# Taps of the shift read in place as fp32, and all steps of a hand-scheduled kernel in another order

## Chip, cores and metric

One core of one Trainium2 chip. The time is device microseconds of one execution, and the median over runs is compared.

## The reference

Two blocks follow each other on one sequence of S = 2048 positions and D = 512 channels (F = 1792 in the MLP). Cut to what is computed:

```python
def _A_ref(q, k, v, shift_k, ssm_k, ssm_D):          # q is already normalised
    for t in range(4):                               # a shift of k by 0..3 positions, 4 taps per channel
        k_shift += k_pad[:, t:t + S, :] * shift_k[:, 3 - t]
    kv = k_shift * v
    y = irfft(rfft(pad(kv)) * rfft(pad(ssm_k)))[:S]  # a causal convolution as long as the sequence
    return q * (y + kv * ssm_D)

def _B_ref(x, w1, w2, w3, w4):
    h = gelu(layernorm(x) @ w1)
    hs = concat(four channel groups of h, moved by -1, +1, -2, +2 positions) @ w2
    x1 = x + hs
    return x1 + gelu(layernorm(x1) @ w3) @ w4

def reference(...):
    h = x + _A_ref(layernorm(x), A_k, A_v, A_shift_k, A_ssm_k, A_ssm_D)
    return h + _B_ref(layernorm(h), B_w1, B_w2, B_w3, B_w4)
```

Inputs and output are bf16. The four taps per channel, `shift_k`, are what the first part of the change is about.

## The kernel before

The kernel is a list of 812 steps. Each is added with a name, the engines that may run it with a planner's cost, the steps it depends on, and the buffers that it takes and gives back (`Plan.add`). A string `ORDER` lists them: a word such as `093P2` is step number 93, on engine P, in buffer 2. `emit` runs through it and issues each step's instructions. So `ORDER` alone sets, for each engine's queue, the order of its instructions, which of several possible engines a step is on, and which buffers it uses. Engines run their queues strictly in order; a step waits in its queue for what it depends on, and all behind it wait too. P is TensorE (PE), V is VectorE (DVE), A is ScalarE (ACT), G is GpSimd (POOL), and S is SyncE (SP), which issues every DMA. The SP queue goes round eight semaphores, so that a transfer is issued only when the one eight places before it has landed.

Positions are split in two halves s = 0, 1 of 8 blocks b of 128 partitions; channels in four chunks c of 128. PSUM has eight banks, handed out by number. The steps in the order of the computation, with their lines in the profile:

- Loads (L268): `Lf` the filter, `Lk` the shifted input k with the taps behind its columns, `Lv`, `Lq`, `Lw1` to `Lw4` the weights. `Lsd` (L273) and `dr` (L296) put `ssm_D` into the filter.
- `skf(c)` (L259, `copy`): casts the four bf16 taps of chunk c, from the last columns of the `Lk` tile in `r_k`, into an fp32 tile `sskf`. `dg(c)` (L309 on DVE, L307 on ACT): four multiplies of the identity by one tap each, which makes four diagonal matrices in `r_dg`.
- `K(g,c)` (L444): seven matmuls with the diagonal matrices, the shift. `KV(g,c)` (L452, DVE): times v.
- `bits` (L324 to L328, DVE), `cons` (L331 to L335, POOL), `ftv`, `fta`, `ft`, `ttv`, `tta`, `tts`, `f2v`, `f2a`, `f2s`: tables of sines, made from indices on POOL, DVE and, last, ACT (L346, L360, L368). `tt` and `f2` finish them on POOL.
- The convolution is a transform in two stages with matrices. `S1` (L391) and its copies out of PSUM `E1` (L259, ACT or DVE), a regrouping of partitions by DMA `X` (L407), `S2` (L415) and its copies `E2` (L259; L427 for the signal F1). The signals are F0, F1 (filter) and A0, A1 (kv). `P` (L476, DVE): products of two spectra in SBUF. `I2` (L486), copies `EV` (L259), DMA `XI` (L497) and `I1` (L504): the way back.
- `Q` (L508) statistics of q for the first layernorm; `QV` (L516 and after), `QP` (L531) and `QN` (L537): mean and inverse deviation on DVE or POOL. `Y` (L614, L616): q normalised, into one of two buffers `z_t`. `H` (L619, DVE): the gated sum h, read from the PSUM of `I1`.
- Per pair p of blocks: `HS` squares (L603 on ACT, L605 on DVE), `uw`, `rr`, `hn` (from L587 to L649) the two layernorm factors, `hb` (L656, L658) the normalised block, `LT` and `TE` its transpose (L673 on PE and a copy L259, or, for some pairs, out and back by DMA, L666 and L668), `W` (L702) times w1, `U` (L706) gelu.
- `X2` (L725) times w2 with the moved groups, `S` (L728), squares `SS` (L603, L605), `ux`, `r1`, `xn` (L587 to L595 and L748 to L759) the third layernorm, `lb` (L656, L658), `LX` and `EX` its transpose in the same two ways, `R` (L732) the residual.
- `M` (L780) times w3 and `G` (L784) gelu, seven of each per pair; `O` (L793) times w4, 14 matmuls per block; `Z` (L795) the last addition and `OUT` (L797) the store.

The taps and their use before:

```python
add(("skf", c), {V: 0.17, GP: 0.22, A: 0.22},
    lambda e, sl, c=c: copy(e, sskf[:, 4 * c:4 * c + 4], kw[:, 0, c, NB * 129:KW]), [("Lk", 0, c)])
...
sc = sskf[:, 4 * c + j:4 * c + j + 1]
...
add(("dg", c), {V: 0.8, A: 1.19, GP: 1.45}, dg(c), [("skf", c)], port="VG")
```

Of the kernel before, what the change touches and what calls it, by code (L numbers as in the profile page):

```python
# [9 lines left out]
P = 128  # L10
# [3 lines left out]
DC = D // P  # L14
FC = F // P
NB = 8
XW = 258
KW = NB * 129 + 4

BF16 = mybir.dt.bfloat16  # L20
F32 = mybir.dt.float32
# [7 lines left out]
SC = 2.0 * math.pi / 4096.0 * (1.0 - 2e-8)  # L29

ORDER = """
002S 004S 003S 005S 031V 041V 042G 043G 000S 029P0 030P 059P23 001S 007S 061P45 006S 062V 067P67 010S 033V 037V 032V 069P01 008S 070V 009S 060A 068A
034V 063P23 064A 065P45 066A 023S 049G 022S 038A 035V 091P60 039V 055P23 099P71 100V 036A 044V 056A 057P45 058A 040V 101P0 102V 103P1 104V 050V 045A
355V 051A 046G 047V 105P7 106V 048A 093P2 095P3 076S 119P45 120A 094V 115P01 354V 077S 054G 024S 075S 015S 096V 097P7 078S 116A 074S 073S 092V 098V
020S 071S 358V 121P23 122A 117P45 107P01 357V 053G 108A 118V 072S 111P67 113P23 021S 114V 016S 127S 109P01 112A 110A 123S 088P4567 089V 128S 090A
085P0123 087A 082P4567 083A 356V 086V 231P21 084A 079P4501 232V 124S 080V 081A 129S 125S 131P6723 130S 134P0145 132V 133A 136A 126S 144V0 143V1 352V
147V2 146V3 135A 014S 137P2367 019S 233P4 011S 139A 018S 145P01670 154V0 153V1 138A 148P 157V2 149A 156V3 223P50 224V 150A 155P01231 158P 159M 160A
187P67 353V 344S 229P5 234V 163V0 164V1 017S 151S 152S 230V 012S 351V 188A 140P0123 141A 235P4 142A 166V2 167V3 161S 162S 165P67010 168P 173V0 013S
359G 169A 174V1 227P5 170A 171S 172S 176V2 175P23671 177V3 178P 180A 199P01 228V 237P5 179V 236V 200A 181S 182S 238V 225P6 226V 343S 360G 361G 052A
362V0 191P23 193P01 192A 189P45 190A 194V 204S 203S 195P67 196A 201P23 202V 197P01 198A 183P45 239P67 365G1 366V 371G1 367A 207S 241P23 208S 184P01  # L40
363V 368G0 364A 242V 243P45 245P23 240A 369V 386G 372V 244A 246A 210S 373A 374V0 209S 206S 205S 257S 387G 185P67 247P01 377V1 375V 380G0 248A 378V
214P2345 215V 370A 249P67 250A 379A 388G 399V 186P01 381V 027S 255S 389G0 392G1 251P23 252A 253P67 254A 376A 383G1 390P00 393P2 259S 216V 211P4567
394V 391A 395P3 258S 384V 212V 382A 220P0145 400G 401G 402A2 405A3 403P21 404A 346S 213V 412G 413G 221V 406P6 397P7 347V 396A 263P0123 385A 398A 407V
265A 260S 222V 408P6 276V0 414G 415G0 416P72 264A 418G1 410P4 425V 426G 417A 411A 419P5 420V 217P0123 409A 275V1 423P7 424A 421P5 219V 277P67230 218V
279V2 427G 428G2 431G3 429P40 422A 534P5 430A 432P0 433A 278V3 535V 536A 282V0 530P1 531V 532A 256S 281V1 436P4 280P 284V2 434P5 435A 437A 285V3 283P
286P 287A 288A 586V 587G 292V0 588G 291V1 522P0 523V 524V 266P4567 526P1 527V 529V 268A 589G0 592G1 262S 590P01 538P2 593P3 594V 528A 537V 591A 542P6
543V 267A 595P70 596A 293P01451 607P3 345S 608A 599P6 603P7 295V2 601P3 539V 294V3 600A 025S 439V 296P 297V0 298V1 300V2 301V3 026S 299P 540A 307V0
544A 643G 442V 605P2 604A 302P 602A 644G 645G 649A2 646V3 597P6 606A 541V 308V1 303A 533V 615G 616G 598A 647P72 304A 443V 261S 269P0123 271V 270A
612P6 613V 272P4501 274V 289S 290S 311V2 310V3 650P2 651V 609P3 610V 648A 309P67010 652P20 312P 617V 653A 656P3 619A0 314V0 028S 445V 273A 657A 618V1
305S 306S 664P2 665A 313V1 316V2 317V3 315P 324V0 318P 319A 620S 654P4 323V1 621S 326V2 662P5 325P23671 327V3 330V0 329V1 622S0 328P 320A 321S 322S  # L50
658P0 663A 333V2 659A 660P1 614S 332V3 331P 661A 655A 438V 440V 444V 334P 335A 669P5 666P0 441V 446V 336A 337S 338S 339P14 623P20 447G 340P36 545V
629P7 448V 452V0 449G1 450V 451A 453V 624A 455G1 456V 341P14 458G0 459V 633P2 454A 473G 474G 631P3 625P6 460V 464A1 461A0 465V 457A 462V 463A 632A
475G 486V 476V3 479V2 635P4 630A 634A 477P11 627P3 466V 498V 348G 636A 478V 626A 470V1 480P7 481A 342P24 628A 487G 488G 482P6 489A1 471V 472A 467G0
468V 469A 490G0 499G 484P7 485A 510V 492S 483A 349V 640P1 491S 550P3 500G 502V3 504S 501A2 503S 493S2 511G 512V 514G0 551V 513A1 515S 546P4 637P2
494P7 496P6 552A 547V 548A 672G 549V 495A 516S 505S0 508P3 506P4 497A 509A 350G 507A 517S1 518P7 519A 520P6 673G 674G 675V3 677S 638V 521A 562P2 676V2
563V 566P3 564A 558P4 567V 554P7 568A 700V 574P6 701G 702G 703A1 704G0 678S 679S2 680P20 611S 705S 570P3 559V 560A 686P4 687A 555V 670V 688P7 692P5
681A 682P4 556V 690P2 575V 576V 553V 683A 684P6 685A 693A 756G 706S 757G 671S 758V 759V3 760G2 707S0 578P4 571V 572V 582P3 728G 729G 583V 730G 731G1
762S 584A 641V 761S 763S1 708P60 710P5 732V0 711A 691A 734S 579V 577V 569V 580V 784V 733S 735S2 785G 525V 557V 639S 720P3 561V 573V 714P1 718P4 719A
709A 764P50 765A 716P2 717A 772P4 766P6 712P5 713A 767A 786G 788G2 790S 787V3 789S 791S0 736P20 737A 768P5 689A 746P6 747A 738P2 739A 642S 774P7 773A
769A 776P6 744P2 667V 668S 777A 740P0 745A 792P40 748P5 796P6 793A 770P2 804P4 797A 800P6 749A 802P5 771A 741A 798P2 715A 801A 805A 803A 742P0 743A  # L60
794P1 694P6 753P4 799A 750P5 775A 778P0 781P2 782V 751V 783S 779V 780S 581V 795A 721A 754V 755S 565V 585V 697P7 698V 695V 699S 809P1 810V 811S 696S
722P3 723V 724S 806P2 807V 808S 725P5 726V 752S 727S
"""


class Plan:
# [28 lines left out]
def body(ctx, tc, fx, kt, q, v, sd, w1, w2, w3, w4, out):  # L95
# [34 lines left out]
    kw = r_k[:].rearrange("p (s c x) -> p s c x", s=2, c=DC)  # L130
# [123 lines left out]
    add, got = plan.add, plan.got  # L254
    A, V, PEc, SP, GP = "A", "V", "P", "S", "G"
    on = {A: act, V: vec, GP: pool}

    def copy(e, o, i):
        (act.copy if e in "AM" else on[e].tensor_copy)(o, i)  # L259
# [34 lines left out]
    add("wend", {PEc: 0.01}, lambda e, sl: None, drop=[("warm", 0)])  # L294
    add("f1", {V: 0.01}, lambda e, sl: None)
    add("dr", {V: 0.5}, lambda e, sl: vec.tensor_tensor(out=fxs[0][0:1, 0, :], in0=fxs[0][0:1, 0, :], in1=drow[0:1, :], op=ADD), ["Lsd", ("Lf", 0, 0)], port="V")  # L296
    for c in range(DC):
        add(("skf", c), {V: 0.17, GP: 0.22, A: 0.22}, lambda e, sl, c=c: copy(e, sskf[:, 4 * c:4 * c + 4], kw[:, 0, c, NB * 129:KW]), [("Lk", 0, c)])

    def dg(c):  # L300
        def f(e, sl):
            for j in range(4):
                sc = sskf[:, 4 * c + j:4 * c + j + 1]
                if e == GP:
                    pool.tensor_scalar(out=diag[:, c, j, :], in0=ident[:], scalar1=sc, scalar2=0.0, op0=MUL, op1=ADD)
                elif e == A:
                    act.activation(diag[:, c, j, :], ident[:], ACT.Copy, scale=sc)  # L307
                else:
                    vec.tensor_scalar(out=diag[:, c, j, :], in0=ident[:], scalar1=sc, scalar2=None, op0=MUL)  # L309
        return f  # L310
    for c in range(DC):
        add(("dg", c), {V: 0.8, A: 1.19, GP: 1.45}, dg(c), [("skf", c)], port="VG")

    sv = small("sv", 8, F32)
    kf = small("kf", 8, F32)
# [530 lines left out]
```

## Time and profile before

| | |
|---|---|
| median of 3 runs | 216.35 us (215.51 to 217.98) |
| the profiled execution | 216.0 us, span 214.2 us, clock 0.996 |
| PE busy | 198.7 us (93% of the span), 1,980 matmuls |
| DVE busy | 147.9 us (69%), 331 instructions |
| ACT busy | 128.3 us (60%), 210 instructions |
| POOL busy | 72.3 us (34%), 194 instructions |
| DMA | 32.85 MB, mean 153 GB/s |

Times in the profile count from the span's start. A share of busy time is a mean over stages with different limits, so the table says which engine has the most work and not which one sets the time at a given place; for that the rows by stage are read. PE's busy time is modelled for pipelined matmuls. Where a row ends in brackets, they hold the idle time of that engine just before it and what ended it.

### The profile page before, as it was taken

To read this page: it belongs to the slowest core of one execution; us is meant where nothing else is said; L and a number is where in the kernel's file an instruction comes from. 1 tells how busy PE (TensorE), PEld (TensorE's weight loads), DVE (VectorE), ACT (ScalarE), POOL (GpSimd) and SP (SyncE) were. 2 spreads that over 40 slices of the span, in tenths; PEclk is the share of its full clock that TensorE was granted. 3 is DMA by queue.
4 is the path that set the end of the run, shared out by engine and by line. 5 is a ranking of instruction groups with operands and counts; after the bars stand their busy time and mean duration, and the time that the engine had idled before them with its cause. 6 is when DMAs were issued, how large, how long until landed. Compare 5 with 4: busy or idle time off the path is not lost.

```text
span 214.2 us, 5136 instructions
## 1 busy us (share of the span) xinstructions
PE 198.7 (93%) x1980; PEld 114.8 (54%) x1980; DVE 147.9 (69%) x331; ACT 128.3 (60%) x210; POOL 72.3 (34%) x194
## 2 busy tenths in 40 slices
PE   7699858898979999999999999799999999999993
PEld 5254324342246646644655774466788887444441
DVE  7999998998999999889894985318687000005621
ACT  4678987889999676961960896345445757000000
POOL 7943000593786436400005883304615000000000
PEclk9999999999999999999999999999999999999998
DMA  6999699978679965030553015850644400000212
GB/s 197 343 386 340 251 362 329 231 203 296 244 252 300 408 249 150 0 100 1 77 148 101 2 23 113 163 122 13 160 99 104 117 2 0 3 0 24 97 50 73
DMA packets 30809, 32.85 MB, mean 153 GB/s; under 512 B 20545, under 2 KB 22594, under 8 KB 30530
## 3 DMA queue, kind: packets, MB, share of 16 engines
q1 hardware_dynamic: 30786, 32.54, 50.0%
q8 instruction: 15, 0.25, 0.5%
q14 instruction: 8, 0.07, 0.1%
HBM read 13.13 MB, written 4.46 MB: 82 GB/s over the span
## 4 chain that ended last, share of the span: by engine, by line
PE 73%; ACT 9%; DMA 7%; issue 4%; DVE 3%; SPq 3%; DVEq 0%; ACTq 0%
PE ps L780 23%; PE ps L793 21%; PE ps L725 6%; PE ps L702 6%; PE ps L486 6%; ACT r_a L259 3%; PE ps L444 3%; DMA r_dg<-dhb 2%; PE ps L504 2%; DMA r_fx<-in_fx_dram 2%; PE ps L415 2%; ACT r_z L259 2%; PE ps L391 2%; ACT junk L603 2%; DMA r_z<-r_vs 2%
## 5 line engine op out<-in xcount | busy, mean ns | idle before, releaser
L780 PEld LDWEIGHTS <-r_k 128*128 128x128 bf16 x448 | 43.2, 98 | 9.4 <-issue 3.2
L795 DVE TENSOR_TENSOR r_v<-ps,r_v 128x512 bf16<-128x512 f32 x16 | 10.7, 687 | 39.4 <-issue 31.4
L780 PE MATMUL ps<-r_dg,r_k 128*128 128x256 bf16 x280 | 32.9, 273 | 0.0
L476 DVE TENSOR_TENSOR r_p<-r_a,r_f 128x1024 bf16<-128x1024 bf16 x48 | 30.7, 685 | 2.5 <-PE ps L486 1.9
L259 ACT CAST r_a<-ps 128x1024 bf16<-128x1024 f32 x25 | 24.2, 1021 | 1.2 <-PE ps L391 0.6
L780 PE MATMUL ps<-xtx,r_k 128*128 128x256 bf16 x168 | 20.2, 273 | 0.0
L728 DVE SCALAR_TENSOR_TENSOR r_q<-r_v,hrr,ps 128x512 bf16<-128x512 bf16 x16 | 11.8, 741 | 9.0 <-PE ps L725 8.9
L444 PE MATMUL ps<-r_dg,r_k 128*128 128x256 bf16 (+3 forms) x112 | 16.0, 288 | 2.1 <-ACT r_f L259 1.7
L486 PE MATMUL ps<-r_p,ttab 32*64 32x512 bf16 x384 | 15.6, 383 | 1.2 <-DVE r_p L476 0.5
L259 ACT CAST r_vs<-ps 128x1024 bf16<-128x1024 f32 (+1 forms) x14 | 14.5, 1075 | 3.2 <-PE ps L486 2.3
L444 PEld LDWEIGHTS <-r_k 128*128 128x128 bf16 x112 | 9.3, 98 | 11.0 <-issue 5.6
L702 PEld LDWEIGHTS <-r_fx 128*128 128x128 bf16 x128 | 12.2, 98 | 5.4 <-issue 1.5
L751 POOL TENSOR_TENSOR xrr<-xrr,mhalf 128x2 f32<-128x2 f32 x8 | 7.0, 876 | 20.4 <-DVE xrr L748 20.0
L784 ACT ACTIVATE r_v<-ps 128x512 bf16<-128x512 f32 x14 | 8.0, 596 | 9.7 <-PE ps L780 9.6
L702 PE MATMUL ps<-r_dg,r_fx 128*128 128x256 bf16 x96 | 11.8, 273 | 1.7 <-DMA r_dg<-dhb 1.2
L603 ACT ACTIVATE junk<-r_v 128x512 bf16<-128x512 bf16 x14 | 9.0, 642 | 6.8 <-DVE r_v L619 5.9
L793 PE MATMUL ps<-w4s,r_kv 128*128 128x512 bf16 x56 | 12.7, 379 | 0.0
L619 DVE SCALAR_TENSOR_TENSOR r_v<-ps,qsd,z_t 128x512 bf16<-128x512 f32 x16 | 11.4, 746 | 1.9 <-PE ps L504 1.6
L793 PE MATMUL ps<-w4s,r_v 128*128 128x512 bf16 x56 | 12.6, 379 | 0.0
L793 PE MATMUL ps<-w4s,r_a 128*128 128x512 bf16 x56 | 12.2, 379 | 0.0
L793 PE MATMUL ps<-w4s,r_f 128*128 128x512 bf16 x56 | 12.2, 379 | 0.0
L391 PEld LDWEIGHTS <-f 128*32 128x32 bf16 x256 | 5.6, 96 | 11.7 <-issue 7.0
(182 smaller groups left out, 353.9 us busy)
## 6 DMA issues: line engine op xcount, KB each, us to landing
r_z<-r_vs SPq DMA_DIRECT2D x16, 256.0 KB, 3.5
r_k<-in_kt_dram SPq DMA_DIRECT2D x8, 259.0 KB, 5.0
r_v<-in_v_dram SPq DMA_DIRECT2D x4, 512.0 KB, 6.3
r_q<-in_q_dram SPq DMA_DIRECT2D x8, 256.0 KB, 6.3
r_f<-r_f SPq DMA_DIRECT2D x8, 256.0 KB, 4.9
r_a<-r_a SPq DMA_DIRECT2D x8, 256.0 KB, 3.0
r_f<-r_a SPq DMA_DIRECT2D x8, 256.0 KB, 3.1
r_a<-r_z SPq DMA_DIRECT2D x8, 256.0 KB, 6.2
```

The source lines that it names most:

```text
L259: (act.copy if e in "AM" else on[e].tensor_copy)(o, i)
L444: nc.tensor.matmul(o[:, (d + j0) * P:(d + j1 + 1) * P], lhsT=kT[s][c][:, bb, x:x + P], rhs=diag[:, c, j0:j1 + 1, :].rearrange("p j x -> p ...
L476: on[e].tensor_tensor(out=prs[:, sl[0], :, :], in0=sp[a][:, kl, t, :, :], in1=gv, op=MUL)
L486: nc.tensor.matmul(ps[64 * t:64 * t + 64, bk[h], :], lhsT=ttab[32 * h:32 * h + 32, 2 * kl + t, 2 if x else xx, :], rhs=prs[32 * h:32 * h + ...
L603: act.activation(junk[:], x, ACT.Square, accum_out=sq[:, i, 1:2])
L619: vec.scalar_tensor_tensor(out=h_sb[s][:, b, :], in0=ps[:, got(("I1", s, b // 2))[b % 2], :], scalar=qsd[:, i:i + 1], in1=z_t[:, got(("Y", ...
L702: nc.tensor.matmul(ps[:, sl[0], j * 256:(j + 1) * 256], lhsT=w1s[:, k, m * P:(m + 1) * P], rhs=xt[:, k, :], start=(k == 0), stop=(k == DC ...
L725: nc.tensor.matmul(ps[:, sl[0], :], lhsT=h1T[s][:, m, bb, x:x + P], rhs=w2s[:, m, :], start=(m == 0), stop=(m == DC - 1))
L728: vec.scalar_tensor_tensor(out=q_sb[:, s, b, :], in0=h_sb[s][:, b, :], scalar=hrr[:, 4 * s + b // 2, 0, b % 2:b % 2 + 1], in1=ps[:, got((" ...
L780: nc.tensor.matmul(ps[:, sl[0], j * 256:(j + 1) * 256], lhsT=w3s[:, k, fc * P:(fc + 1) * P], rhs=xt[:, k, :], start=(k == 0), stop=(k == D ...
L793: nc.tensor.matmul(ps[:, sl[0], :], lhsT=gb[:, fc, (b % 2) * P:(b % 2 + 1) * P], rhs=w4s[:, fc, :], start=(fc == 0), stop=(fc == FC - 1))
L795: add(("Z", s, b), {V: 0.61}, lambda e, sl, b=b: vec.tensor_tensor(out=h_sb[s][:, b, :], in0=ps[:, got(("O", s, b))[0], :], in1=h_sb[s][:, ...
```

## The change

The taps lie in the `Lk` tile as fp32 instead of bf16. The host puts each bf16 tap into the upper half of a 32-bit word whose lower half is zero, which is the same number in fp32; the tile's rows grow from 1036 to 1040 bf16 columns. `dg` reads its scalar from there. The steps `skf` and the tile `sskf` are gone, so 808 steps are left, and every step added after them has a number that is lower by four. `ORDER` is another list throughout.

```diff
-KW = NB * 129 + 4
+KW = NB * 129 + 8
...
-    sskf = ct("sskf", DC * 4, dt=F32)
...
-    for c in range(DC):
-        add(("skf", c), {V: 0.17, GP: 0.22, A: 0.22}, lambda e, sl, c=c: copy(e, sskf[:, 4 * c:4 * c + 4], kw[:, 0, c, NB * 129:KW]), [("Lk", 0, c)])
...
-                sc = sskf[:, 4 * c + j:4 * c + j + 1]
+                sc = r_k[:, c * KW + NB * 129:(c + 1) * KW].rearrange("p (o x) -> p o x", o=1)[:, 0, :].bitcast(F32)[:, j:j + 1]
...
-        add(("dg", c), {V: 0.8, A: 1.19, GP: 1.45}, dg(c), [("skf", c)], port="VG")
+        add(("dg", c), {V: 0.8, A: 1.19, GP: 1.45}, dg(c), [("Lk", 0, c)], port="VG")
...
-    taps = _np.broadcast_to(a["A_shift_k"].reshape(DC, P, 4), (2, DC, P, 4))
-    kt = _np.concatenate([kt, taps.astype(kt.dtype)], axis=3)
+    taps = _np.zeros((2, DC, P, 4, 2), kt.dtype)
+    taps[..., 1] = a["A_shift_k"].reshape(DC, P, 4)
+    kt = _np.concatenate([kt, taps.reshape(2, DC, P, 8)], axis=3)
```

The two `ORDER` strings share no line; read with the steps' names, these are the places that matter below (steps in the order of the queue; what is left out is "..."):

```
SP, start
 before Lf01 Lf03 Lf02 Lk00 Lsd Lf00 Lk02 Lk01 Lv01 Lk03 Lv00 Lq02 Lq01 X.F0 ...
 after  Lf02 Lk00 Lf03 Lk02 Lk01 Lsd Lf00 Lk03 Lf01 Lq03 Lv01 Lv00 X.F0 ...
SP, middle: Lw2 stood before XI(0,0); it now stands among the X of A1. The four Lq of s=1
 stood among the X of A1 or later; three of them now stand among the X of F1
DVE, start
 before bits E1 skf0 dg0 dr E1 skf1 skf2 dg2 KV fta dg3 KV KV f2a Q tta KV ...
 after  dg0 bits dr E1 dg1 Q f2v KV fta KV KV KV f2a KV KV tta KV KV ...
ACT, start
 before E1 x4 dg1 skf3 E1 x2 ft f2s tts E1.A0 ...
 after  E1 x5 dg3 E1 x2 ft f2s tts E1.A0 ...
POOL, start
 before cons ftv f2v ttv f2 tt QV0 QP0 QN0 Y01 Y03 ...
 after  dg2 edge0 cons ftv ttv f2 tt QP0 QN0 Y00 Y01 ...
PE, 70 to 90 us before
 before I2(1,0,0..3) X2(0,0) S2.A1(1) X2(0,1) LX02 X2(0,4) LX03 X2(0,5) M(0,1,0) ...
 after  I2(1,0,0..3) X2(0,1) X2(0,4) X2(0,5) LX02 S2.A1(1) LX03 X2(0,0) M(0,1,0) ...
DVE after S(0,2)
 before P P P ux(0,1) P P S(0,0) ...
 after  P P P P P P Q(1,0) R(0,3) ...
POOL after hb(0,6)
 before hb07 r1(0,1) xn(0,1) lb02 lb03 ux(0,0) ...
 after  ux(0,1) r1(0,1) xn(0,1) lb02 lb03 ux(0,2) r1(0,2) ux(0,0) ...
PE after I1(1,3)
 before W(1,0) x2 O05 X2(0,7) X2(0,6) O04 W(1,1) x2 W(1,2) ...
 after  M(0,2,1) LT10 LT11 O05 W(1,0) x2 O04 X2 x2 W(1,1) x2 W(1,2) ...
SP, transposes of s=1
 before LT13 LT12 LT15 LT14 TE12 LT16 LT17 TE14 TE16 ...
 after  LT12 LT13 LT15 TE12 LT14 LT16 LT17 TE14 TE16 ... EX12 LX10 LX16 LX11 OUT05 OUT07 EX10 LX17 EX16 ...
```

Between the engines, 36 steps leave DVE's queue (three of them skf, which are gone) and 33 come to it; the steps on PE and on SP are the same ones in another order. The steps `uw(1,1)`, `hb(1,5)` and `hb(1,6)` are on POOL after the change and were on DVE, DVE and ACT.

## Prediction

> **What bounds the kernel now.** I read the page's second part first, then busy time by stage, then single rows. The columns of the page's rows are 40 slices of 5.35 us each.
>
> ```profile
> PE   7699858898979999999999999799999999999993
> DVE  7999998998999999889894985318687000005621
> ACT  4678987889999676961960896345445757000000
> DMA  6999699978679965030553015850644400000212
> ```
>
> ```profile
> 0.00:17.50 17.50, 14.18 (x149) 7.90 (x149) 15.62 (x51) 11.12 (x18) 12.43 (x64) 1.00 0.89 318
> 17.50:33.50 16.00, 12.41 (x222) 4.99 (x215) 14.93 (x20) 15.12 (x16) 0.86 (x3) 1.00 0.89 302
> 33.50:50.00 16.50, 15.05 (x220) 6.68 (x221) 15.97 (x25) 14.19 (x15) 8.07 (x13) 1.00 0.93 261
> 50.00:62.50 12.50, 10.45 (x120) 3.65 (x119) 12.08 (x30) 12.13 (x23) 9.18 (x22) 1.00 0.65 240
> 62.50:110.00 47.50, 47.39 (x620) 27.56 (x619) 44.10 (x88) 33.58 (x58) 15.74 (x37) 1.00 0.54 173
> 110.00:140.00 30.00, 28.79 (x202) 17.79 (x187) 19.45 (x66) 17.46 (x36) 16.42 (x37) 1.00 0.39 81
> ```
>
> Each stage row has its length, busy us of PE, PEld, DVE, ACT and POOL, PE clock, DMA share, GB/s. Two stages show. Up to 62.5 us DVE is busy for 58.6 us, and ACT and the DMA engines are close behind; PE is busy for 52.1, so about 10 us of PE idle lie there. After 62.5 PE sets the time: its only later hole over a microsecond is the last line of the next fence. So a change in order gains where it brings PE's work after 62.5 forward, and loses where it opens a hole in it.
>
> ```profile
> 6.42 1.53 POOL L343 TENSOR_SCALAR r_a<-r_a,sv 128x512 int32<-128x512 int32 x2
> 6.61 0.61 DVE L259 CAST sskf<-r_k 128x4 f32<-128x4 bf16 x1
> 7.25 1.26 DVE L309 TENSOR_SCALAR r_dg<-ident,sskf 128x128 bf16<-128x128 bf16 x4
> ...
> 39.77 3.68 DVE L476 TENSOR_TENSOR r_p<-r_a,r_f 128x1024 bf16<-128x1024 bf16 x6
> 39.94 3.58 POOL L516 TENSOR_TENSOR qnm<-qst 128x8 f32<-128x8 f32 x1 [21.51 <-DVE qst L508]
> 43.48 0.21 POOL L517 TENSOR_TENSOR qrs<-qst 128x8 f32<-128x8 f32 x1
> ...
> 79.63 1.52 POOL L658 TENSOR_SCALAR r_k<-r_q,xrr,xnm 128x512 bf16<-128x512 bf16 x2
> 80.58 0.39 PE L673 MATMUL ps<-ident,r_k 128*128 128x128 bf16 x4
> ...
> 138.90 3.67 PE L702 MATMUL ps<-r_dg,r_fx 128*128 128x256 bf16 x32 [1.21 <-DMA r_dg<-dhb]
> ```
>
> These are rows of the timeline: start, length, engine, line. A POOL operation on 8 elements took 3.58 us while six DVE products (L476) ran, and the next, alike, 0.21: POOL was held until DVE's run ended. The other way round, the first tap copy and the first multiply behind it stretched while POOL ran L343. At 79.63 POOL makes two normalised blocks (lb); PE transposes the first 0.18 us after it is done: no slack there.
>
> **The copies.** Four skf steps go: 0.61, 0.23 and 0.15 us on DVE, 0.19 on ACT. DVE is nearly full there, so they count, but only in DVE's sum below. The multiply reads a scalar from r_k instead of sskf; no such row exists. Bound: no change to, if the address mattered, the slowest multiply of that line (0.74 against a median of 0.25) 16 times, 8 us spread over three engines; I take nothing: engine, shape and count stay, the row it is nearest to is the median of the same line, and the 0.74 has POOL's L343 beside it. The kt rows grow by 8 bytes in 2,072: below 0.03 us a load.
>
> **DVE's work in the filling stage.** PE's 1,980 matmuls are the same. I went through both orders and added each step's median start-to-start time on its engine. Up to the first pair of H steps (H(0,0), H(0,1); 52.30 us before) DVE has: one PSUM copy less (E1, E2, EV: 11 to 10, -1.13), one dg less (-0.92), three skf less (-0.57 start to start), Y(0,0) gone to POOL (-0.46), f2v come from POOL (+0.5, estimated from 0.5 a POOL operation of the same size) and QV(0) come from POOL (+0.77, its own row for s=1): -1.8. Up to S(0,2), which ended at 75.57, it is -2.7 by the same sums, and up to the last product P it is -2.5. ACT gets 0.8 more before E1 of A0 and 2.6 more by EV(0,3,1), but had 2.5 us idle between 33.3 and 51.3. QV(0) leaves POOL, where it took 4.98 us because of the hold above. The transfers allow it too: Lw2 (0.5 MB) leaves the stretch before 50 us, where they are 0.89 to 0.93 busy at about 300 GB/s, which is 1.7 us. Bounds of the gain by the time of S(0,2): 1.7 and 2.7; I take 2.2. If another engine holds DVE, this is gone (rivals below).
>
> **What takes part of it back.** The step ux(0,1) moves from DVE (0.48 us) to POOL (0.97 to 1.42 for five small operations). It becomes ready just after S(0,2), and DVE then runs six products without a break, 6 x 0.60 = 3.6 us. Held as at 39.94, POOL starts at S(0,2)+3.6, and needs 0.8 more for ux, 1.06 for r1, 0.45 for xn and 0.76 for lb(0,2): S(0,2)+6.7. Queued behind it on POOL are r1, xn, both lb and the whole chain of the next pair; PE's queue waits at LX(0,2), and all of PE behind it. Before, S(0,2) ended at 75.57, so lb(0,2) comes at 82.3 less the gain, and PE would be there at 80.8 less the gain (0.2 later by its own order: one X2 of 0.86 more, one S2 of 0.65 less ahead of it). The wait is 1.5 us if held, nothing if not (ACT's square SS ends 0.9 after S(0,2); with 0.97, 1.06, 0.45 and 0.76 behind it lb(0,2) ends at S(0,2)+4.1, ahead of PE). I take 1.0: L516 is the nearest row, but DVE's runs had breaks of 0.66 and 1.04 for buffers.
>
> The Trainium skill, page "SBUF — State Buffer", section "Who interferes with whom", says that a DVE instruction with two SBUF inputs contends with a GpSimd one that reads SBUF, and that the second waits out the first. The trace agrees: 3.58 against 0.21. By the rule alone the hold would be whole, and the time below 0.5 us longer.
>
> **The hole at 138.90.** PE waits 1.21 us for transposes TE(1,4). Between I1(1,3) and W(1,2), PE now has 13.5 us of work instead of 12.3 (M(0,2,1) and two transposes LT lie behind I1(1,3)). But POOL now has uw(1,1), hb(1,5) and hb(1,6) in that chain (1.35 + 2 x 0.75) and SP's TE(1,2) stands ahead of LT(1,4), with LT(1,6), LT(1,7) and TE(1,4) queued behind it. Bounds: 1.2 gained, 0.4 lost; I take 0.4 gained. Two later transposes, EX(1,0) and EX(1,6), now stand on SP behind an output store, OUT(0,7). Counted from O(0,7)'s start: Z(0,7) ends at 3.9, the store is issued by 4.35, EX(1,0) lands 3.1 later (156.90 to 160.01 before) at 7.45, and PE wants it at 3.02 + 6 x 0.87 = 8.3. EX(1,6) follows lb(1,7) (ends near 6.8) and its store's landing (2.2): 9.1 + 3.1 = 12.2 against 12.6. Both priced at nothing; with the slowest landing seen (4.75, TE(1,4)) they cost 0.9 and 1.3 (the larger counts). The last matmul, its 0.69 us addition and the store are as before.
>
> Sum: 2.2 - 1.0 + 0.4 = 1.6 gained. The profiled execution is 216.0 us, 214.2 of it span; so 214.4. The median of the runs is 0.35 higher, so 214.8 beside 216.35. One per cent, about what can be told from no change here, is 2.2 us.
>
> **Rivals.**
> *The hold does not happen* (POOL slips into DVE's gaps): the whole 2.2 to 2.7 stays, with the 0.4: 213.6. For it: POOL's five ux operations at 82.44 ended within 1.62 us while DVE ran. Against: 3.58 at 39.94.
>
> *The filling stage is set by transfers.* S2 of A0 waits for its three DMA transfers, 2.1 us in the list of waits; they leave SP when ACT finishes E1(A0,0,1), which both orders put sixth among ACT's copies of that stretch. Then DVE's saving turns into DVE waits: 216.2. The lower DMA load (Lw2) speaks against it.
>
> *Slower: the constants come late.* bits now stands behind dg(0) on DVE, and POOL must do dg(2) before cons, ftv and ttv. Lk(0,2) is the fourth load; the fourth landed at 6.6 us, Lk(0,2) itself at 7.9. dg(2) on POOL is unseen: four operations of 0.31 (128x64 elements) to 0.77 (128x512). With 0.38, ttv ends at 6.6 + 1.5 + 1.3 + 1.5 + 3.9 = 14.8, ahead of DVE's tta at about 16: hidden. With 7.9 and 0.77 it ends at 17.7, tta and tts follow at 18.8 against 16.91 before, and ACT, which takes its steps in order and was idle for only 0.6 us from 17.48 to 33.28, starts E1(A0) 1.3 late with 0.8 to 2.6 us more work: 2.1 to 3.3 lost, 219.0. It decides once ttv ends after about 16.
>
> That the change does not do what it says is no rival: the four copies are gone from the instruction lists.
>
> **How the numbers follow.** Forecast 0.44 (213.8 to 215.8), no hold 0.22, transfers 0.16, constants late 0.18. Faster by over 1% (below 214.2): the no-hold case and a quarter of the forecast, 0.33. Slower (above 218.5): nearly all of the last case and a little for holes unseen, 0.19. Same: 0.48. The range leaves out half of the no-hold case's lower part and half of the last: 212.8 to 218.9.
>
> **What would show it.** H(0,0) ends near 50.3 and S(0,2) near 73.4; the first L673 transpose after X2(0,5) waits for POOL by about a microsecond; ux on POOL has one operation of several microseconds; the wait at L702 near 137 is below 1.2; ttv ends by 15 and tts by 17.5. It is wrong if tts is later than 17.5, if PE waits between 65 and 110 anywhere else for over a microsecond, or if EX(1,0) or EX(1,6) opens a hole near 160.

## The result and the profile after

| | before | after |
|---|---|---|
| median | 216.44 us (215.09 to 217.98, 20 runs) | 217.72 us (216.44 to 221.03, 20 runs) |
| ratio to before | | 1.0055, 95% interval 1.0028 to 1.0082 |
| the profiled execution | 216.0 us, span 214.2 | 218.46 us, span 216.7 |

The change makes the kernel slower by about 1.2 us, or 0.55%. The profiled execution after lies 0.74 us above its median and the one before 0.44 below its own, so their difference of 2.5 us is about twice that of the medians; a second profile of the changed kernel, from the run of experiment 10, has a span of 215.7 and is used beside the first below. In some executions of either kernel PE's clock is halved for 3.41 us somewhere (last section): six of the 20 after have a mean clock of 0.981 to 0.992, and their median is 219.5 us against 217.3 for the other 14. Each ratio is to the kernel before on the same chip; the experiments used four chips.

The second part of the page of the changed kernel, and its busy time by stage (length; busy us of PE, PEld, DVE, ACT, POOL; PE clock, DMA share, GB/s):

```profile
PE   7969779997866999999999999799999999999993
DVE  6799989998999697897982887748968100212021
ACT  4786999898996876874670864231840469001500
DMA  6999888986859806844034105942126504002001
```

```profile
0.00:17.50 17.50, 14.12 (x134) 8.02 (x135) 13.63 (x44) 11.29 (x16) 11.74 (x66) 1.00 0.87 299
17.50:33.50 16.00, 13.08 (x221) 5.15 (x227) 15.25 (x21) 14.68 (x17) 1.68 (x4) 1.00 0.86 297
33.50:50.00 16.50, 14.93 (x234) 6.73 (x233) 16.47 (x31) 15.39 (x17) 2.96 (x5) 1.00 0.90 255
50.00:62.50 12.50, 9.89 (x112) 3.33 (x120) 11.37 (x33) 11.75 (x21) 10.13 (x24) 1.00 0.72 260
62.50:110.00 47.50, 44.81 (x596) 26.66 (x597) 41.64 (x84) 34.44 (x59) 26.45 (x49) 1.00 0.55 179
110.00:140.00 30.00, 29.54 (x218) 17.84 (x216) 21.43 (x62) 14.23 (x31) 11.87 (x26) 1.00 0.37 76
```

Up to 62.5 us DVE is busy for 56.7 us instead of 58.6: the saving of the prediction is there. PE's busy time there is the same (52.0 for 52.1): PE got nothing of it. From 62.5 to 110, where PE had been full (47.39 of 47.50), it is now busy for 44.81. The list of waits of the changed kernel for that stretch names them (engine and line, waited for, us in total, times, longest):

```profile
PE ps L411 <- DMA r_a<-r_z: 1.8, 1, 1.8
PE ps L411 <- DMA r_f<-r_a: 1.6, 2, 1.1
PE ps L500 <- DMA r_z<-r_vs: 1.3, 1, 1.3
PE ps L789 <- DMA w4s<-in_w_dram: 0.4, 1, 0.4
PE ps L669 <- POOL r_k L654: 0.4, 1, 0.4
```

The kernel before has no wait for a transfer in the same stretch (49.5 to 110 us). The rows behind it, from the timeline of the changed kernel:

```profile
9.34 1.47 DVE L305 TENSOR_SCALAR r_dg<-ident,r_k 128x128 bf16<-128x128 bf16 x4
...
18.31 0.72 ACT L356 ACTIVATE ttab<-r_a,negpi 128x512 bf16<-128x512 int32 x1 [1.18 <-DVE r_a L355]
...
50.09 1.04 PE L500 MATMUL ps<-r_z,f 128*128 128x512 bf16 x4 [1.28 <-DMA r_z<-r_vs]
...
69.29 0.62 PE L411 MATMUL ps<-r_a,ftab 64*32 64x512 bf16 x16 [1.82 <-DMA r_a<-r_z]
...
78.58 0.52 POOL L589 TENSOR_TENSOR xmv<-xsq 128x2 f32<-128x2 f32 x1
79.18 0.58 POOL L590 TENSOR_TENSOR xmv<-xsq,xmv 128x2 f32<-128x2 f32 x1
...
82.83 0.40 PE L669 MATMUL ps<-ident,r_k 128*128 128x128 bf16 x4 [0.41 <-POOL r_k L654]
...
140.99 1.26 PE L698 MATMUL ps<-r_dg,r_fx 128*128 128x256 bf16 x10 [1.45 <-DMA r_dg<-dhb]
```

And SP's queue alone, from the same view (start, length, transfers issued in a row):

```profile
50.77 2.31 SPq L403 DMA_DIRECT2D r_f<-r_a  x2
53.16 1.03 SPq L267 DMA_DIRECT2D r_q<-in_q_dram  x2
54.26 1.85 SPq L403 DMA_DIRECT2D r_f<-r_a  x3
56.14 1.04 SPq L267 DMA_DIRECT2D r_q<-in_q_dram  x1
57.64 1.18 SPq L403 DMA_DIRECT2D r_f<-r_a  x2
60.12 0.52 SPq L403 DMA_DIRECT2D r_a<-r_z  x1
```

At 50.09 PE comes to I1(0,0) early and waits for XI(0,3), the last transfers of the way back. From 53 us three q loads (r_q) stand on SP among the X.F1 transfers (r_f from r_a), and X.A1 (r_a from r_z) follows: X.F1(1,3) is issued at 57.64 instead of 52.58, X.A1(1,0) at 64.89 instead of 61.38, and S2.A1(0) starts at 69.29 instead of 65.93. The hole at W(1,2), the last line, is 1.45 instead of 1.21.

For every profile I added PE's idle time between its steps in two stretches, from I1(0,0) to I1(1,0) and from there to PE's last matmul (the sum of gaps between one step's last matmul and the next step's first):

| kernel | I1(0,0) starts | to I1(1,0): us, idle | to the last matmul: us, idle |
|---|---|---|---|
| before | 49.71 | 66.54, 1.87 | 94.23, 1.21 |
| old order, taps in place | 50.22 | 66.57, 1.88 | 94.53, 1.33 |
| after, first profile | 50.09 | 67.97, 4.83 | 94.87, 1.77 |
| after, second profile | 49.29 | 67.14, 3.94 | 95.48, 2.30 |
| after, q loads late | 49.25 | 66.73, 3.31 | 95.75, 2.52 |
| the same, S2.A1(0) later | 48.88 | 66.70, 3.12 | 95.36, 2.13 |
| after, less DVE work | 48.65 | 67.16, 4.05 | 95.23, 2.07 |
| all shortened waits (the last edit) | 49.98 | 67.26, 2.93 | 94.93, 1.84 |

So the new order reaches I1(0,0) between 0.4 us later and 0.4 earlier, loses 0.6 to 1.4 us in the first stretch and 0.6 to 1.3 in the second. The lengths count here and not the idle time: the first stretch holds the same steps in both kernels, but PE's busy time for them is 64.7 us before and 63.1 to 63.2 after, so the added idle time (2.1 to 3.0 us) is more than what was lost.

### The profile page after: what moved, and what is told of

It is laid out like the page before. It is cut to its first block, busy times and chain, and to the rows that moved or that the text cites. A ratio compares the mean times of both kernels' runs of the same rounds, so it can differ in the third digit from the quotient of the medians.

```text
span 216.7 us, 5125 instructions
## 1 busy us (share of the span) xinstructions
PE 198.0 (91%) x1980; PEld 114.8 (53%) x1980; DVE 146.2 (67%) x328; ACT 127.8 (59%) x210; POOL 76.9 (36%) x198
## 3 DMA queue, kind: packets, MB, share of 16 engines
q1 hardware_dynamic: 30786, 32.55, 49.5%
## 4 chain that ended last, share of the span: by engine, by line
PE 62%; DMA 16%; ACT 8%; DVE 5%; SPq 4%; issue 2%; POOL 0%; ACTq 0%; DVEq 0%
PE ps L789 23%; PE ps L776 20%; DMA w4s<-in_w_dram 5%; PE ps L698 5%; PE ps L721 4%; PE ps L482 4%; DMA r_a<-r_a 3%; SPq L267 2%; ACT r_z L258 2%; PE ps L500 2%; DMA r_a<-r_z 2%; DMA r_fx<-in_fx_dram 2%; DMA r_z<-r_vs 2%; PE ps L440 2%; DMA r_dg<-dhb 2%
## 5 line engine op out<-in xcount | busy, mean ns | idle before, releaser
L776 PE MATMUL ps<-r_dg,r_k 128*128 128x256 bf16 x336 | 38.7, 273 | 0.0
L780 ACT ACTIVATE r_a<-ps 128x512 bf16<-128x512 f32 x14 | 8.0, 612 | 19.9 <-PE ps L776 19.9
L482 PE MATMUL ps<-r_p,ttab 32*64 32x512 bf16 x384 | 14.5, 382 | 1.0 <-DVE r_p L472 1.0
L258 ACT CAST r_vs<-ps 128x1024 bf16<-128x1024 f32 x15 | 14.6, 1025 | 1.3 <-PE ps L482 1.2
L258 ACT CAST r_f<-ps 128x1024 bf16<-128x1024 f32 x13 | 12.7, 1036 | 4.3 <-PE ps L387 3.8
L612 POOL TENSOR_SCALAR z_t<-r_q,qrs,qnm 128x512 f32<-128x512 bf16 x9 | 9.0, 1003 | 15.0 <-DVE r_v L615 11.9
L780 ACT ACTIVATE r_f<-ps 128x512 bf16<-128x512 f32 x14 | 7.8, 605 | 10.9 <-PE ps L776 10.9
L527 POOL TENSOR_TENSOR qrs<-qsd,mhalf 128x8 f32<-128x8 f32 x2 | 3.3, 1650 | 29.1 <-DVE qsd L522 29.1
L776 PE MATMUL ps<-xtx,r_k 128*128 128x256 bf16 x112 | 13.2, 273 | 0.0
L728 DVE SCALAR_TENSOR_TENSOR r_v<-r_q,hnm,r_v 128x512 bf16<-128x512 bf16 x16 | 12.5, 798 | 0.1
```

What stands on the lines that cost most here:

```text
L482: nc.tensor.matmul(ps[64 * t:64 * t + 64, bk[h], :], lhsT=ttab[32 * h:32 * h + 32, 2 * kl + t, 2 if x else xx, :], rhs=prs[32 * h:32 * h + ...
L612: on[e].tensor_scalar(out=z_t[:, sl[0], :], in0=qs, scalar1=qrs[:, i:i + 1], scalar2=qnm[:, i:i + 1], op0=MUL, op1=ADD)
L728: vec.scalar_tensor_tensor(out=h_sb[s][:, b, :], in0=q_sb[:, s, b, :], scalar=hnm[:, 4 * s + b // 2, 0, b % 2:b % 2 + 1], in1=h_sb[s][:, b ...
L776: nc.tensor.matmul(ps[:, sl[0], j * 256:(j + 1) * 256], lhsT=w3s[:, k, fc * P:(fc + 1) * P], rhs=xt[:, k, :], start=(k == 0), stop=(k == D ...
L780: act.activation(gb[:, 2 * fp:2 * fp + 2, :], ps[:, got(("M", s, p, fp))[0], :].rearrange("p (j x) -> p j x", j=2), ACT.Gelu_apprx_tanh)
```

## The experiments

Moves are given by the steps' names in one engine's queue.

**1. The taps alone.** The order of before, with the four skf words taken out and the numbers behind them lowered by four; twice.

> The part alone: the taps are read as fp32 in place and the four copies skf are gone, but every step keeps the order, engine and buffers of the kernel before. Theory A (the new order costs the time, the taps do not): 0 to 0.9 us faster than before (0.61 + 0.23 + 0.15 us of copies leave DVE, where the opening chain has no gaps), ratio 0.996 to 1.000; the dg multiplies keep their median of 0.25 us on DVE. Rival (the scalar read in place slows the multiplies): ratio above 1.002 and dg rows longer than before by more than 0.1 us each.

> The taps read in place in the old order, once more, to narrow its interval (1.0025, 0.9998 to 1.0052). If reading in place costs: 1.002 to 1.003 again. If the first value was chance, and the copies' removal is neutral: 0.999 to 1.001. A gain of 0.5 us or more (0.9975 or less) is what the prediction's sum held for the copies.

Measured: 1.0025 (0.9998 to 1.0052), and on another chip 0.9986 (0.9953 to 1.0019). Together nothing: the first value was chance as far as these runs tell. The dg multiplies are as before: in dg(2) and dg(3) on DVE each takes 0.23 to 0.25 us in both kernels (dg(0) took 1.54 us here and 1.26 there, both beside larger operations on POOL). In the first of the two, K(3,2) waited 1.0 us for a load of k, which led to the next run.

**2. The longer rows alone.** The order and the copies of before.

```diff
-KW = NB * 129 + 4
+KW = NB * 129 + 8
... (skf still copies four columns; the host adds four columns of zeros)
```

> The kernel before with nothing changed but the row length of the kt loads: 2,080 bytes instead of 2,072, as in the changed kernel, by four unused elements; the tap copies stay. Theory E (the longer, differently aligned rows make the loads land later, as K(3,2)'s wait of 1.0 us for Lk(1,2) in the run of the old order suggests): ratio 1.002 to 1.004. Rival (the row length is nothing; landings differ from execution to execution by as much): ratio within 0.0015 of 1.

Measured: 0.9985 (0.9959 to 1.0011). The row length is nothing; landings differ from execution to execution by as much as that wait. As far as these three runs tell, the loss is in the order.

**3. Is DVE what bounds the filling stage?** In the changed kernel:

```diff
-        return lambda e, sl: vec.bn_stats(qst[:, 8 * s + b, :], q_sb[:, s, b, :])
+        return lambda e, sl: vec.bn_stats(qst[:, 8 * s + b, :], q_sb[:, s, b, 0:64 if s == 0 else D])
```

> The changed kernel with the statistics Q(0,0) to Q(0,7) taken over 64 of the 512 elements of each row, which takes about 8 x 0.45 = 3.6 us of DVE work out of the stretch from 10.9 to 45.3 us and changes nothing else. It asks if DVE work saved in the filling stage is time saved, as the prediction's sum took it. Theory C (what ends the stage is the chain from I2(0,3) over ACT's copies EV(0,3) and the transfers XI(0,3), which wait for products only in part): I1(0,0) and H(0,0) come at most 1 us earlier than in the other runs of this order (I1(0,0) at 48.9 to 50.1) and the ratio stays within 0.003 of 1.0055. Rival (DVE bounds the stage): H(0,0) comes 2.5 us or more earlier, near 47.5, and the ratio falls to 0.995 or less.

Measured: 1.0030 (0.9982 to 1.0078). The eight rows went from 0.684 to 0.214 us, 3.8 us of DVE work gone; H(0,0) ended at 50.12, against 51.56 and 50.77 in the changed kernel's two profiles: 0.6 to 1.4 us for 3.8. Even that is no more than the scatter, since H(0,0) ended between 50.36 and 53.17 in the other profiles of this order. PE's wait at I1(0,0) for the transfers stayed (timeline of this run):

```profile
48.65 1.04 PE L500 MATMUL ps<-r_z,f 128*128 128x512 bf16 x4 [1.22 <-DMA r_z<-r_vs]
```

Theory C holds: in this order DVE does not set the end of the filling stage. I1(0,0) waited for XI(0,3) in all but one of the profiles of this order, 0.95 to 2.46 us. The same was not tried in the order of before, where PE did not wait there.

**4. The q loads and S2.A1(0).** First the loads alone, then with one step moved on PE.

```diff
 SP, changed kernel
-X.F1(1,1) Lq(1,0) Lq(1,3) X.F1(0,2) X.F1(1,0) X.F1(1,2) Lq(1,1) X.F1(1,3) ... X.A1(1,1) Lw3
+X.F1(1,1) X.F1(0,2) X.F1(1,0) X.F1(1,2) X.F1(1,3) ... X.A1(1,1) Lq(1,0) Lq(1,3) Lq(1,1) Lw3
 PE, second run
-S2.A1(0) W(0,2,0) W(0,2,1)
+W(0,2,0) S2.A1(0) W(0,2,1)
```

> The changed kernel with three q loads, Lq(1,0), Lq(1,3) and Lq(1,1), issued behind the last X.A1 transfer (ahead of Lw3) instead of among the X.F1 transfers. Theory A (the q loads hold back X.F1 and, through the rotation of SP's eight semaphores, X.A1): X.F1(1,3) is issued near 54.5 instead of 57.64, the PE wait of 1.14 us at S2.F1(3) goes, X.A1(1,0) is issued near 63.6 instead of 64.89, S2.A1(0) starts near 68.0 instead of 69.29, and the time falls by about 1.2 us: ratio to before 0.998 to 1.002 where the changed kernel has 1.0055. Rival (ACT's copies E1.A1, late by 1.6 us, set X.A1 and the loads do not matter): S2.A1(0) stays within 0.4 us of 69.29 and the ratio stays at 1.004 to 1.007.

> The changed kernel with the q loads late as in the run with late q loads, and with S2.A1(0) placed behind W(0,2,0) on PE, so that PE has 0.87 us of other work while it lands. Theory A: both waits together were 1.14 + 1.82 us; with the loads late and PE's work ahead, S2.A1(0) waits 0.8 us or less, and X2(0,3) starts near 71.5 instead of 73.63; 2.0 us gained against the changed kernel: ratio to before about 0.996 (0.993 to 0.999). Rival (PE's work after it is held by DVE or POOL instead, which got nothing earlier): the wait moves to LX(0,2) or to the products and the ratio is 1.000 or more.

Measured: 1.0032 (1.0000 to 1.0064) and 1.0030 (0.9997 to 1.0063). The X.F1 transfers came as theory A had them: X.F1(1,3) issued at 53.94 and 53.86. The waits of the second of these runs from 49.5 to 110 us no longer name X.A1 (r_a from r_z):

```profile
PE ps L669 <- DVE nbx L654: 0.6, 1, 0.6
PE ps L411 <- DMA r_f<-r_a: 0.5, 1, 0.5
PE ps L669 <- POOL r_k L654: 0.5, 1, 0.5
```

From I1(0,0) to I1(1,0) both take 66.7 us, as before the change (66.54) and 0.4 to 1.3 less than the changed kernel's two profiles. But the median fell by 0.5 us where 1.2 and 2.0 were expected, and these intervals overlap that of the changed kernel (1.0028 to 1.0082), so the times alone do not show a gain. The moved S2.A1(0) added nothing beyond the loads, and part of what is won comes back at W(1,2), whose hole is 2.20 and 1.81 in these two profiles.

The traces say what the loads did. Times in us from the start of I1(0,0):

| | before | after, first profile | after, second profile | q loads late |
|---|---|---|---|---|
| X.F1(1,3) issued | 2.87 | 7.55 | 7.53 | 4.69 |
| E1.A1(3,1) ends on ACT | 11.65 | 12.86 | 12.87 | 12.87 |
| X.A1(1,0) issued | 11.67 | 14.80 | 14.12 | 14.10 |
| X.A1(1,0) landed | 13.97 | 19.16 | 18.52 | 18.35 |
| S2.A1(0) starts | 16.23 | 19.20 | 18.56 | 18.49 |

With the loads late, X.F1(1,3) is issued 2.9 us sooner. That gains nothing at S2.F1(3): PE waits there for 1.14, 0.36 and 0.31 us in the three profiles of the new order, but LT(0,2), the next step on PE, starts at 13.0 in all three. S2.A1(0) comes 0.71 us sooner than in the first profile and only 0.07 sooner than in the second. In the first, the landing of the last X.F1 (63.01) releases X.A1(0,0) (63.02) and with it the transfers behind it on SP; in the second and with the loads late, ACT's copy E1.A1(3,1) is the last to be done, and X.A1(1,2), X.A1(0,3) and X.A1(1,0) follow it in a row. So theory A is right for X.F1 and for the first profile, and its rival, the late copy on ACT, for the other two. With the loads late X.A1(1,0) still lands 4.4 us later than before: 1.2 by the copy, 1.2 by the two transfers that now stand ahead of it, 2.0 by a longer landing. No run moved these three.

**5. One copy on DVE again.** E1.A1(0,1) on DVE behind E2.F1(1,1), on ACT in the changed kernel.

> The changed kernel with the one copy E1.A1(0,1) on DVE (behind E2.F1(1,1)), as before the change, instead of ACT. Theory A (the q loads set it): E1.A1(3,1) ends about 0.9 us earlier on ACT (62.0 instead of 62.95), but the X.A1 transfers still wait for the landing of X.F1, S2.F1(3) still waits about 1.1 us, S2.A1(0) starts within 0.5 us of 69.29, and the ratio stays at 1.004 to 1.008 (DVE has 1.2 us more work). Rival (the late ACT copies set it): S2.A1(0) starts 0.9 us earlier and the ratio falls to about 1.001.

Measured: 1.0057 (1.0030 to 1.0084), no change, as theory A had it. But the run does not test the rival: on DVE the copy came 7.8 us after the start of I1(0,0) (2.5 before the change), S1.A1(3,0) now waits 1.08 us, and ACT's last copy E1.A1(3,1) ended no sooner, 13.1 us after I1(0,0) against 12.9.

**6. The hole at W(1,2), by SP's order.**

```diff
 SP, changed kernel
-LT(1,5) TE(1,2) LT(1,4) LT(1,6) LT(1,7) TE(1,4)
+LT(1,5) LT(1,4) TE(1,2) LT(1,6) LT(1,7) TE(1,4)
```

> The changed kernel with one SP step moved: the store LT(1,4) is issued ahead of the transpose TE(1,2), as before the change, instead of behind it. Theory B (SP's order makes the hole at W(1,2): TE(1,2) waits for LT(1,3)'s landing and LT(1,4) stands behind it): LT(1,4) is issued about 1.4 us earlier relative to I1(1,0), TE(1,4) lands as much earlier, the hole of 1.45 us at W(1,2) shrinks to 0.3 or less, W(1,1) starts at most 0.4 later, and the time falls by 1.0 to 1.4 us: ratio to before 0.998 to 1.001 where the changed kernel has 1.0055. Rival (POOL's normalised blocks hb(1,5) and hb(1,6) set it, or TE(1,6) inherits the wait): the hole stays at 1.0 us or more or moves to W(1,3), ratio 1.004 or more.

> The run with late q loads and S2.A1(0) behind W(0,2,0), with LT(1,4) ahead of TE(1,2) in addition. In the run without the latter the hole at W(1,2) was 1.81 us (1.45 in the changed kernel), so what was won at S2.F1(3) and S2.A1(0) came back there in part. Theory A + B: the hole is 0.6 us or less and the time is 1.2 to 1.6 us below that run's 216.82, 215.4: ratio to before 0.995 to 0.998. Rival (something behind W(1,2) on DVE, POOL or the transposes is late whatever comes before): the time stays at 216.4 or more, ratio 1.001 or more, with a new wait at W(1,3), X2(1,x) or LX(1,x).

Measured: 1.0121 (1.0072 to 1.0171) and 1.0076 (1.0016 to 1.0135). Theory B falls in this form. LT(1,4) was issued 1.34 us earlier after I1(1,3), but TE(1,4) only 0.5, since it still stands behind LT(1,6) and LT(1,7), which wait for hb(1,6), made on POOL at 133.72 to 134.50; and it then took 4.97 us to land instead of 3.81. The hole was 2.10 and 2.24. In both profiles PE's clock is halved behind it, seen in the busy time by windows of the first of them (columns as above):

```profile
137.24:140.65 3.41, 1.31 (x13) 0.94 (x11) 3.23 (x11) 1.33 (x3) 0.38 (x1) 1.00 1.13 124
140.65:144.06 3.41, 3.41 (x17) 2.43 (x18) 0.87 (x3) 0.00 (x0) 0.69 (x3) 0.50 0.42 92
144.06:147.47 3.41, 3.41 (x25) 2.12 (x23) 0.56 (x1) 1.76 (x4) 0.00 (x0) 1.00 0.37 77
```

PE is busy for 1.31 of 3.41 us, and in the 3.41 us behind that its clock is 0.50: half the work in that window, so about 1.7 us more (an estimate, half of 3.41), in the part of the kernel that PE sets. Four of the six executions of each run had a mean clock under 0.995, and so had five of 11 of the kernel before on that chip; how much of the two medians this makes is not shown.

**7. All of it, with ux(0,1) on DVE and Lw4 right behind Lw3.**

> The run before this one in the list with two more edits: ux(0,1) on DVE (behind the third product of that run) instead of POOL, and Lw4 issued right behind Lw3. Expected by the traces so far: ux(0,1) takes 0.5 us on DVE, r1(0,1) starts about 1.3 us earlier, the wait of 0.41 to 0.46 us at LX(0,2) goes, and O(0,3) no longer waits (0.43 in the changed kernel). 0.4 to 0.8 us below the run before it, ratio to before about 0.994 (0.991 to 0.997). Rival (the products that DVE makes 0.5 us later are what I2(1,1,0) waits for): LX(0,2) has no wait, but the same time is lost at I2(1,1,0) or at S2.A1(1), and the ratio equals that of the run before it.

Measured: 1.0099 (1.0054 to 1.0144). The hole was 2.41, and the clock fell behind it again. The part on ux(0,1) is told by the trace up to there: r1(0,1) started 2.45 us after the end of S(0,2) instead of 3.81, the waits at LX(0,2) and O(0,3) were gone, and M(0,1,0) still started 8.14 us after S(0,2) instead of 8.18. The rival is right here: ux(0,1) on POOL cost nothing that stayed.

**8. Work in the hole.** The changed kernel, and the run before with all edits, with

```diff
+                if (s, p, h) == (1, 2, 0):
+                    for i in range(20):
+                        nc.tensor.matmul(ps[:, sl[0], 0:P], lhsT=ident[:], rhs=ident[:], start=True, stop=True)
```

> The changed kernel with 20 extra 128x128 matmuls of the identity put on PE ahead of W(1,2,0), into the PSUM bank that W(1,2,0) then overwrites: about 1.1 us of work in the hole of 1.45 us, with no result used. Theory D (a hole of about 2 us inside one of the clock's windows of 3.41 us halves PE's clock for the next window, which costs about 1.7 us just where PE sets the end; in the traces so far the clock fell at W(1,2) behind holes of 2.10, 2.24 and 2.41 us, and not behind 1.45 and 1.58): W(1,2,0) starts no earlier, the profile is as before, but no run has a halved window there: runs with a mean clock under 0.995 are rarer than the 6 of 20 of the changed kernel and lie within 1.2 us of its others, not 2.2 above them; the median falls by 0.3 to 0.6, ratio 1.003 to 1.005. Rival (the clock falls at random and the hole has nothing to do with it): as many runs at 219 us and above, ratio 1.0055 or more by what the extra matmuls cost.

> The run with all four edits (218.33, with the clock halved for one window behind its hole of 2.41 us) with the same 20 extra matmuls in that hole. Theory D: PE's idle time there is at most 1.3 us at a stretch, the clock stays whole from 138 to 150 us in the profile and in nearly all runs; median 216.2 to 216.8, ratio to before 1.000 to 1.003. Rival (random): median stays at 218 or more, with runs at a mean clock of 0.99.

Measured: 1.0104 (1.0055 to 1.0153) and 1.0092 (1.0056 to 1.0128). The second of them, from its timeline:

```profile
137.12 1.28 PE L696 MATMUL ps<-ident 128*128 128x128 bf16 x20
139.44 1.80 PE L701 MATMUL ps<-r_dg,r_fx 128*128 128x256 bf16 x15 [1.04 <-DMA r_dg<-dhb]
```

The hole was filled and neither profile has a halved window there (in the first, PE now waits 1.0 us at M(1,3,0) instead). But the medians, 219.39 and 218.28, did not come down to what was expected. In the first, each of its six executions had a mean clock of 0.990 to 0.992, one halved window; in the one that was profiled it lies at 33.22 to 36.63 us. In the second, six of eight executions kept the whole clock, and their median is still 218.05. So the hole at W(1,2) is one place where the clock falls and not the reason that the changed kernel is slower. Why all six of the first had such a window is open: on the same chip the kernel before had one in two of 19.

**9. A shorter chain ahead of W(1,2), and the copy EV(0,3,0) on DVE.**

```diff
 the run with all edits, DVE
-H(1,4) hn(1,0) ... uw(1,2) edge1 H(1,7) TE(1,0) hb(1,2) Y(1,6) H(1,6) R(0,4) hb(1,4) uw(1,3)     (uw(1,1) on POOL)
+H(1,4) uw(1,1) hn(1,0) ... uw(1,2) hb(1,2) edge1 H(1,7) TE(1,0) Y(1,6) H(1,6) hb(1,4) uw(1,3) R(0,4)
 SP: LT(1,3) ahead of LT(1,2)
 second run, in addition: EV(0,3,0) on DVE ahead of Q(0,2), E1.F1(2,0) on ACT, XI(0,3,1) ahead of XI(0,3,0)
```

> The run with all four edits (no extra matmuls), with the chain ahead of W(1,2) shortened: uw(1,1) on DVE as before the change instead of POOL, hb(1,2) ahead of H(1,7) on DVE, hb(1,4) and uw(1,3) ahead of R(0,4), and the store LT(1,3) ahead of LT(1,2). Theory B (the hole at W(1,2) is set by the stretch H(1,x) to uw, rr, hn, hb to the store, and then by two transposes of about 4 us each that follow one another): TE(1,2) is issued about 1.5 us earlier after I1(1,3) than in the run with all four edits (+7.9 us), the hole falls from 2.41 to under 1 us, with no halved window behind it: median 215.3 to 216.0, ratio to before 0.996 to 1.000. Rival (the transposes' own time on the DMA engines sets it, so TE(1,6) inherits the wait): W(1,3) waits as long as W(1,2) did, ratio 1.003 or more.

> All edits so far that shortened a wait (q loads late, S2.A1(0) behind W(0,2,0), LT(1,4) ahead of TE(1,2), ux(0,1) and uw(1,1) on DVE, Lw4 early, the shorter chain ahead of W(1,2)), and in addition the copy EV(0,3,0) on DVE beside EV(0,3,1) on ACT, with E1.F1(2,0) on ACT in exchange and XI(0,3,1) issued ahead of XI(0,3,0). Expected: both XI(0,3) transfers are issued by 2.0 us after I2(0,3,1) ends (2.05 to 2.6 in the other runs of this order), I1(0,0) waits 0.3 to 0.6 us less, and executions without a halved window take 215.8 to 216.2; ratio to before 0.997 to 1.002. If the transfers' landing (3.7 to 5.4 us) swamps that, I1(0,0) waits as before and the ratio is that of the run before it, 1.0038.

Measured: 1.0038 (1.0002 to 1.0075) and 1.0079 (1.0044 to 1.0114). TE(1,2) came 6.9 us after I1(1,3) instead of 7.9 and the hole fell to 1.49 and 1.52. The edit brings uw(1,1) back to DVE and moves three other steps at once, so it does not say which of them did it, and the rest of the hole stays. In the second run XI(0,3) was issued by 1.8 us after I2(0,3,1) ended, as expected, and PE no longer waited at I1(0,0), but only because it came there later itself: I1(0,0) started 6.3 us after I2(0,3,1) ended, as in the changed kernel (6.2 and 6.1). No kernel in this order was faster than before. In the first of the two, the six executions of 12 with a whole clock have a median of 216.44 us, against 216.28 for those of the kernel before on that chip; the other six have 219.18. Sorted like this, after the fact, most of what this version still loses is the halved clock.

**10. The changed kernel again,** as the yardstick on the chip of the last ones.

> The changed kernel itself on the same chip as the three others, as their yardstick: 1.0055 (1.003 to 1.008) as in the first comparison. If this chip halves PE's clock more often, more than 6 of 20 executions have a mean clock under 0.995 and the ratio is up to 1.010.

Measured: 1.0077 (1.0041 to 1.0114). The first comparison stands.

## Why the prediction was wrong

**The sign, and the term that failed.** The forecast was 214.8 us, 1.6 faster; measured 217.72, 1.2 us slower, inside the range of 212.8 to 218.9. The step that failed is "DVE's work in the filling stage ... I take 2.2". Its first half is right (DVE had 1.9 us less up to 62.5 us). Its second half, that DVE's saving is PE's, is not: H(0,0) ended at 51.56 and 50.77 instead of 50.3 (52.30 before), so 0.7 to 1.5 of the 2.0 us came through on DVE; but PE reached I1(0,0) at 50.09 and 49.29 (49.71 before), and S(0,2) ended at 76.63 and 75.19 instead of 73.4 (75.57 before). Experiment 3 shows why: 3.8 us less on DVE brought H(0,0) at most 0.6 to 1.4 us. In the new order the chain over PE, ACT's copies and the transfers XI(0,3) ends last there; the copy EV(0,3,0), on DVE before and beside EV(0,3,1), now stands ahead of it on ACT. I had the sign against it in hand: DVE's share in a stage says that it is full, not that its last step is what PE waits for.

**The transfers rival** (216.2, 0.16) had the mechanism and the wrong place. I looked at S2 of A0 and at Lw2, which left the stretch before 50 us, and did not follow where Lw2 and three q loads went: into SP's queue among X.F1 and X.A1. The front part of this document lists that move. Its own mechanism, a late copy on ACT that holds back transfers, is what the trace shows one signal further on, at E1.A1(3,1) and X.A1 (experiment 4). As a loss the move of the loads and of the copies should have been priced there: the first stretch of the table is 0.6 to 1.4 us longer. With the loads late 0.4 to 1.3 us of that were gone, but only 0.07 to 0.71 at S2.A1(0), so how much the loads cost is not settled.

**The hold on POOL,** 1.0 us, was mis-sized. ux(0,1) took 2.07 us while DVE ran its products, its longest operation 0.58 us, not 3.58; PE waited 0.41. What failed is the hold over the whole run of products: its four POOL operations came through between 78.29 and 80.36 at 0.21, 0.52, 0.58 and 0.51 us, with products of two SBUF inputs on DVE from 77.76 to 80.31. The rule that I cited from the Trainium skill, "SBUF — State Buffer", section "Who interferes with whom", speaks of one instruction that waits out another, and the trace fits that: none of the four took longer than one product (0.60 us). Why one operation at 39.94 took as long as six products is open. Experiment 7 puts what stayed of it at nothing.

**The hole at W(1,2)** was to shrink to 0.8 and was 1.45 and 1.82: the wrong side of bounds of 1.2 gained and 0.4 lost, and in the second profile outside them. uw(1,1), hb(1,5) and hb(1,6) on POOL were named against it; with uw(1,1) back on DVE and three steps reordered it came down from 2.41 to 1.49. One move in that chain was not named: hb(1,2) went from ACT to DVE and starts 2.8 us after I1(1,3) ends, where it was 0.1, and the store LT(1,3), which TE(1,2) needs, is issued 4.7 us after I1(1,3) starts instead of 1.6. That SP's order alone does it is refuted (experiment 6).

**The constants.** ttv ended at 14.30 as forecast, but tts at 19.03, later than the 17.5 that was to show the prediction wrong: DVE's own queue was late (dr waited 1.19 us for a load; dg(1) took 1.47 us beside POOL where dg(0) took 0.74). In the second profile it was 17.63, and in other runs of the same opening 17.13 to 18.48. Of the 1.40 us between the two profiles 0.80 were left at I1(0,0). So the rival's mechanism is possible, and its 2.1 to 3.3 us too much; two profiles do not show that the constants made the 0.80.

**Right:** the scalar read in place costs nothing (no change within 0.3%; of the 0.57 us that the sum held for the copies, the two runs together show nothing either), no hole at EX(1,0) or EX(1,6), and the tail: 3.72 us from PE's last matmul to the end before, 3.77 after.

What stays open: 0.3 to 0.4% between the kernel before and the best repaired versions of the new order (1.0030, whose interval reaches 1, and 1.0038, whose interval begins at 1.0002). Part may be the rest of the hole at W(1,2), a wait of 0.32 us at X2(1,7) that the old order lacks, and the clock: on the four chips 31 of 93 executions of the kernel before had a mean clock under 0.995, and 53 of 103 of the kernels in the new order. The rest was not taken apart.

## What to carry to other kernels

A stage in which an engine is 94% busy, as DVE is here, is bound by it only if the step that the next stage waits for ends that engine's queue: halve some of its work in a run of its own before crediting what it saves. When a new order takes loads out of one stretch, find the place where they are put back, and list what stands behind them in the queue that issues them. A wait that a trace names is worth what the next step starts later by: count steps from a common point in two profiles before a wait is given a price, as in the table of experiment 4. One profile can be off by more than the effect: here two profiles of the same kernel differ by 1.4 us at tts and by 0.9 in PE's idle time between I1(0,0) and I1(1,0).

## What the runs showed of the hardware

PE's clock falls to one half for exactly one window of 3.41 us, at multiples of 3.41 us from where it first rose. In the 17 profiles, each of the five windows in which PE was idle for 2.10 us or more was followed by a halved one; the next below, 1.82 us idle, was not (windows of the changed kernel):

```profile
67.16:70.57 3.41, 1.59 (x26) 0.83 (x25) 3.41 (x7) 1.67 (x4) 3.07 (x6) 1.00 0.95 354
70.57:73.98 3.41, 3.41 (x45) 2.44 (x44) 1.47 (x3) 3.41 (x7) 1.12 (x2) 1.00 1.01 392
```

Three more halved windows came behind 1.26, 1.26 and 1.67 us of idle time, all between 21 and 34 us, where PE runs small tiles (64 by 32 and 32 by 64); 28 others with 1.26 to 1.82 us were not followed by one. Whether a given hole falls into one window or is cut in two changes from execution to execution: in the run with late q loads a hole of 2.20 us lay across a border, and the clock stayed whole. The Trainium skill, "TensorE: Matmul & The Clock Gate", Part 1, has a free-running window of 3.4 us and a clock that goes to half after an idle one; the trace agrees on the window, and here 62% of one idle (2.10 of 3.41 us) was enough.

A second thing not expected: the same transfer, XI(0,3,1), landed 3.8 to 4.3 us after its issue in eleven of the twelve profiles where PE waited for it and 5.3 in the other, and 3.5 to 3.6 in the four profiles of the old order. One late landing is as large as the whole effect measured here.
